# Bringing and summing K and V of the first two batches one batch at a time in a pooled-attention and top-1 MoE kernel

## The chip, the core and the metric

The kernel runs on one core of a Trainium2 chip. Time is device time in microseconds (us) of one execution. The engines are TensorE (PE for matmuls and transposes, PEld for weight loads), VectorE (DVE), ScalarE (ACT), GpSimd (POOL) and SyncE (SP); DMAs are issued from SP, ACT and POOL.

## The reference

```python
# q, k, v: (8 batches, 8 heads, 576 rows, 64)
k_p = k.reshape(B, H, 72, 8, D).mean(axis=3)        # 8 rows become one
v_p = v.reshape(B, H, 72, 8, D).mean(axis=3)
attn = softmax(scale * q @ k_p.transpose(0, 1, 3, 2))
x = (attn @ v_p).transpose(0, 2, 1, 3).reshape(4608, 512)
expert = argmax(x @ w_gate)                         # 8 experts, top-1, limited capacity
out[i] = gate_w[i] * (relu(x[i] @ w1[expert]) @ w2[expert])
```

## The kernel before

**Stages.** The first stage (some 150 us) is attention, in 36 units of work; the rest is the mixture of experts, which the change does not touch. A unit is 256 query rows (two blocks of 128) of four heads. Batch 0 has units 0 to 3, unit 4 holds the last 64 rows of batches 0 and 1 together (the tail unit), units 5 to 8 are batch 1, and so on. The loop over n issues, for unit n: its scores on PE (L476, L479), maximum and subtraction on DVE (L486, L491), the exponential on ACT (L494); for unit n-2: the transposes of its exponentials (L502, copied out by ACT at L503), the products with V (`av`, L516) and their scaling on DVE (`norm`, L525 to L540); for unit n+1 the transposes of its q (`q_part`, L462, copied out at L463). Each engine works through its instructions in the order in which they are written, so an instruction that waits holds up all behind it.

**Pooling K and V.** K and V come for pairs of batches. A pair's 1152 groups of 72 rows lie in 128 partitions, 9 sums to be made in each, and three DMAs of 768 KB bring three sums' rows each (`load_third`). The sums are made by POOL in three additions (`tree`, L370 to L374) or by DVE in one reduction (`red`, L380). For the first pair both engines share them; all later pairs are POOL's. The raw rows lie in 7 buffers.

**Preparing a batch.** `prep_k(b)` transposes the sums of K on PE (L408) into one PSUM bank, and ACT copies them (L417) into `kbs[b % 2]`, which the scores read. `prep_v(b)` does the same for V into `vT` and in a second step multiplies (L438) and masks (L440, L442) into `vbd[b % 2]`, which `av` reads. `turns(n)` says in which unit they are issued: batch 1's K in unit 1 and V in units 2 and 3, batch 2's K in unit 5, V in units 7 and 8.

**The start.** Before unit 0, PE has nothing to do; `busy` gives it products of zeros (L266). K of batches 0 and 1 is summed, batch 0's K prepared, unit 0's q transposed. V's last sums and `prep_v(0)` fall into units 0 to 2. POOL fills its constant tables (`setup`, of which `rest` is the later part) between sums.

**DMA issue.** DMAs from SP and ACT take turns on eight completion semaphores. A ninth DMA is issued only when the one that had its semaphore before has landed. At the start the eight are three of K, one of q, and four small ones of the gate weights (`wgi`, issued from ACT).

Of the kernel before, what the change touches and what calls it, by code (L numbers as in the profile page):

```python
# [31 lines left out]
def pooled_attn_top1_moe(ctx: ExitStack, tc: tile.TileContext, q, k, v, wg, w1, w2, cap, out):  # L32
# [129 lines left out]
    with ExitStack() as actx:  # L162
# [31 lines left out]
        def load_kv(p):  # L194
            raws[p] = [[early_k if p == 1 and src is k and i == 0 else load_third(src, p, i) for i in range(3)] for src in (k, v)]
# [28 lines left out]
        rk = [load_third(k, 0, i) for i in range(3)]  # L224
        qb[0] = ld.tile([P, H, NB, D], F32, name="qblk", tag="qblk")
        rv = []
        for f in range(2):
            hs = slice(f * HH, (f + 1) * HH)
            src = q[0, hs, 0 : NB * P, :].rearrange("h (p j) d -> p h j d", j=NB)
            for j in range(0, NB, 2):  # L230
                nc.sync.dma_start(qb[0][:, hs, j : j + 2], src[:, :, j : j + 2])
                if f == 0:
                    rv.append(load_third(v, 0, j // 2))
            if f == 0:
                rv.append(load_third(v, 0, 2))
        raws[0] = [rk, rv]
        early_k = load_third(k, 1, 0)
# [31 lines left out]
        nc.vector.tensor_copy(wgi[:, :, 0:D], ident[0:D, None, 0:D].to_broadcast([D, NCH, D]))  # L269
# [9 lines left out]
        for i in range(2):  # L279
            nc.vector.tensor_scalar(out=vbd[i][:, :, :, XW - 1 : XW], in0=mk[:, :, :, None], scalar1=float(POOL), scalar2=None, op0=ALU.mult)  # L280
# [109 lines left out]
        def pool(p):  # L390
            for w, dst in (("k", kps[p]), ("v", vps[p])):
                left[w, p] = 3
                for i in range(3):
                    gq.append(tree(dst[:, third(i)], raws[p]["kv".index(w)][i], (w, p)))
                    if p == 1 and w == "k" and i == 0:
                        gq.append(rest)

        def turned(x, b, w, z=None):

            while left.get((w, b // 2)):  # L400
# [342 lines left out]
        with tc.manual_schedule():  # L743
            nc.gpsimd.memset(kbs[1], 0.0)
            z = busy(33)
            rest = setup()
# [488 lines left out]
```

## Time and profile before

| | us |
|---|---|
| median of 3 runs (627.95 to 629.42) | 629.0 |
| the profiled execution | 628.05 |
| its span, first to last instruction | 626.3 |

The profiled execution's time is 1.75 us more than its span. Busy times are shares of the span; a unit of the attention takes 4 to 5 us. In timelines each row is a start, a duration (merged over consecutive instructions of one kind, where x says how many), engine, line, tiles written and read, and in brackets the idle time of the engine before it with what ended it.

### The profile page before, as it was taken

To read this page: it belongs to the slowest core of one execution; us is meant where nothing else is said; L and a number is where in the kernel's file an instruction comes from. 1 tells how busy PE (TensorE), PEld (TensorE's weight loads), DVE (VectorE), ACT (ScalarE), POOL (GpSimd) and SP (SyncE) were. 2 spreads that over 40 slices of the span, in tenths; PEclk is the share of its full clock that TensorE was granted. 3 is DMA by queue.
4 is the path that set the end of the run, shared out by engine and by line. 5 is a ranking of instruction groups with operands and counts; after the bars stand their busy time and mean duration, and the time that the engine had idled before them with its cause. 6 is when DMAs were issued, how large, how long until landed. Compare 5 with 4: busy or idle time off the path is not lost. (4 is left out here: it accounts for less than half of the span.)

```text
span 626.3 us, 14918 instructions
## 1 busy us (share of the span) xinstructions
PE 609.2 (97%) x4249; PEld 549.1 (88%) x4250; DVE 304.2 (49%) x680; ACT 262.2 (42%) x443; POOL 302.1 (48%) x468
## 2 busy tenths in 40 slices
PE   9999999999999999999999999999999999999993
PEld 8889899898898888988888989989899888988982
DVE  4667877978878212168265622118212674112112
ACT  2565576577561212268274522217212582212122
POOL 7799779355644241345544441345414255341344
PEclk9999999999999999999999999999999999999997
DMA  9998963394722520158627820224502271120121
GB/s 322 351 351 305 349 205 115 127 264 146 269 83 71 185 67 14 53 174 310 195 100 273 296 103 5 64 67 139 204 34 67 76 253 40 64 67 18 49 66 51
DMA packets 47084, 93.81 MB, mean 150 GB/s; under 512 B 13392, under 2 KB 23632, under 8 KB 47060
## 3 DMA queue, kind: packets, MB, share of 16 engines
q1 hardware_dynamic: 30836, 60.37, 28.0%
q0 software_dynamic: 11392, 21.57, 11.3%
q10 hardware_dynamic: 4832, 11.56, 5.1%
q8 instruction: 14, 0.23, 0.2%
q14 instruction: 10, 0.08, 0.0%
HBM read 132.97 MB, written 31.27 MB: 262 GB/s over the span
## 5 line engine op out<-in xcount | busy, mean ns | idle before, releaser
L1141 DVE SCALAR_TENSOR_TENSOR hl<-ph,hh 128x512 fp32r<-128x512 f32 x60 | 40.7, 690 | 145.8 <-ACT hh L1140 134.2
L1140 ACT ACTIVATE hh<-ph 128x512 fp32r<-128x512 f32 x60 | 36.0, 599 | 115.8 <-PE ph L150 115.8
L150 PE MATMUL ph<-xh,w1h 128*128 128x256 f32 x480 | 76.4, 282 | 2.4 <-DVE hl L1141 1.8
L150 PE MATMUL ph<-xh,w1l 128*128 128x256 f32 x480 | 75.8, 280 | 0.0
L150 PE MATMUL ph<-xl,w1h 128*128 128x256 f32 x480 | 75.8, 280 | 0.0
L95 POOL DMA_INDIRECT xg<-xs,ix x42 | 45.9, 1094 | 56.7 <-PE y L159 49.2
L159 PE MATMUL y<-w2h,hh 128*128 128x512 f32 x280 | 71.7, 398 | 0.0
L150 PEld LDWEIGHTS ph<-xh,w1h 128*128 128x128 f32 x480 | 65.7, 189 | 4.7 <-DVE hl L1141 2.6
L159 PE MATMUL y<-w2h,hl 128*128 128x512 f32 x280 | 69.3, 390 | 0.0
L159 PE MATMUL y<-w2l,hh 128*128 128x512 f32 x280 | 69.2, 389 | 0.0
L516 PE MATMUL pa<-vbd,pT 96*128 96x146 f32 (+1 forms) x480 | 66.4, 294 | 0.8 <-DVE lt L540 0.8
L150 PEld LDWEIGHTS ph<-xl,w1h 128*128 128x128 f32 x480 | 65.2, 190 | 0.0
L150 PEld LDWEIGHTS ph<-xh,w1l 128*128 128x128 f32 x480 | 64.7, 189 | 0.0
L159 PEld LDWEIGHTS y<-w2l,hh 128*128 128x128 f32 x280 | 52.6, 188 | 11.1
L159 PEld LDWEIGHTS y<-w2h,hl 128*128 128x128 f32 x280 | 52.6, 188 | 10.9
L516 PEld LDWEIGHTS pa<-vbd,pT 96*128 96x128 f32 (+1 forms) x480 | 56.4, 179 | 4.4 <-DVE lt L540 1.9
L100 POOL DMA_INDIRECT out_dram<-zrow,iz x40 | 50.6, 1264 | 15.5 <-issue 15.5
L159 PEld LDWEIGHTS y<-w2h,hh 128*128 128x128 f32 x280 | 49.6, 188 | 9.6 <-ACT hh L125 0.9
L126 DVE TENSOR_TENSOR xl<-px,xh 128x512 fp32r<-128x512 f32 x40 | 25.8, 686 | 60.8 <-ACT xh L125 60.8
L93 POOL TENSOR_TENSOR guard<-ix 128x2 int32<-128x2 int32 x21 | 4.1, 194 | 104.8 <-DVE ix L90 100.4
L125 ACT CAST xh<-px 128x512 fp32r<-128x512 f32 x40 | 21.5, 591 | 73.8 <-PE px L1128 73.5
L676 POOL DMA_INDIRECT slots<-pairs,gix x36 | 35.5, 986 | 33.4 <-DVE pairs L669 19.9
(236 smaller groups left out, 1052.1 us busy)
## 6 DMA issues: line engine op xcount, KB each, us to landing
r<-in_moe_w_dram SPq DMA_DIRECT2D x84, 1024.0 KB, 7.5
raw<-in_k_dram SPq DMA_DIRECT2D x12, 768.0 KB, 9.8
raw<-in_v_dram SPq DMA_DIRECT2D x12, 768.0 KB, 9.5
xs<-xo ACTq DMA_DIRECT2D x16, 512.0 KB, 5.0
qblk<-in_q_dram SPq DMA_DIRECT2D x14, 512.0 KB, 8.5
raw<-in_moe_w_dram SPq DMA_DIRECT2D x4, 512.0 KB, 5.0
r<-in_moe_w_dram ACTq DMA_DIRECT2D x2, 1024.0 KB, 8.5
qblk<-in_q_dram SPq DMA_DIRECT2D x4, 256.0 KB, 8.7
```

Source lines behind the costliest of these rows:

```text
L93: nc.gpsimd.tensor_sub(guard[:, :, 0:1], ix[:, :, 0:1], ix[:, :, 0:1])
L95: nc.gpsimd.indirect_dma_start(out=dst[:, i, :].bitcast(F32), out_offset=None, in_=src, in_offset=bass.IndirectOffsetOnAxis(ap=ix[:, i, 0: ...
L100: ins = nc.gpsimd.indirect_dma_start(out=out[:, :], out_offset=bass.IndirectOffsetOnAxis(ap=i_, axis=0), in_=src, in_offset=None, bounds_c ...
L125: nc.scalar.copy(hi, src)
L126: eng.tensor_sub(lo, src, hi.bitcast(F32))
L150: nc.tensor.matmul(p[:, f2], a[:, c, f * P : (f + 1) * P], b[:, c], start=(f2 == 0 and j == 0 and c == 0), stop=(f2 == 1 and j == 2 and c ...
L159: nc.tensor.matmul(y, a[:, c, i * P : (i + 1) * P], b[:, c], start=(n == 0), stop=(n == 3 * KF - 1))
L516: nc.tensor.matmul(self.pa[us, j, h0 * XW : (h0 + 2) * XW], self.pT[:, j, c, us], vbd[b % 2][:, cc].rearrange("r a x -> r (a x)"), start=( ...
L676: ins = nc.gpsimd.indirect_dma_start(out=slots[:, :], out_offset=bass.IndirectOffsetOnAxis(ap=ix[:, g, 0:1], axis=0), in_=pairs[:, pr + g0 ...
L1140: nc.scalar.activation(hh[s], p, AF.Relu)
L1141: nc.vector.scalar_tensor_tensor(out=hl[s], in0=p, scalar=0.0, in1=hh[s].bitcast(F32), op0=ALU.max, op1=ALU.subtract)
```

## The change

K and V of batches 0 and 1 are loaded and summed per batch. A batch's 64 groups (head and eighth of the rows) have nine sums each; the first eight are laid over 128 partitions, sums 0 to 3 in even and 4 to 7 in odd partitions, in two DMAs of 512 KB, and the ninth lies in 64 partitions, in one DMA of 128 KB. The order of the loads becomes K0, a quarter of q0, V0, a quarter of q0, K1, two quarters of q0, V1. The sums lie in `kps[-2]`, `kps[-1]` for batches 0 and 1, and `turned` and `natural` have a second form for them: three transposes in place of five, three copies in place of two. For batch 0's K, ACT copies partitions 0 to 63 of the bank and DVE partitions 64 to 127. `prep_k(1)` moves from unit 1 to unit 3, `prep_v(1)` from unit 2 to 4, `prep_k(2)` from 5 to 7, `prep_v(2)` from 7 to 8. Two preparations of constants move from DVE to ACT. `rest` goes behind the sums of K and V of batches 2 and 3. The dummy products before unit 0 fall from 33 to 19, and q of unit 0 is transposed ahead of K.

```diff
+        def load_one(src, b):
+            view = src[b].rearrange("h (g r j) d -> (h g) r (j d)", r=NR, j=POOL)
+            four = view[:, 0 : NR - 1].rearrange("q (a r) x -> q a r x", a=2)
+            ts = [kv_tile() for _ in range(2)]
+            for i, t in enumerate(ts):
+                nc.sync.dma_start(t[:, 0:2], four[:, :, 2 * i : 2 * i + 2])
+            nc.sync.dma_start(ts[1][0:GB, 2:3], view[:, NR - 1 :])
+            return ts
...
+        one["k", 0] = load_one(k, 0)
+        load_first_q(0, 0)
+        one["v", 0] = load_one(v, 0)
+        load_first_q(0, 2)
+        one["k", 1] = load_one(k, 1)
+        for j in range(0, NB, 2):
+            load_first_q(1, j)
+        one["v", 1] = load_one(v, 1)
         load_qtail(0)
         load_q(1)
...
-        nc.vector.tensor_copy(wgi[:, :, 0:D], ident[0:D, None, 0:D].to_broadcast([D, NCH, D]))
+        nc.scalar.copy(wgi[:, :, 0:D], ident[0:D, None, 0:D].to_broadcast([D, NCH, D]))
...
+            if b < 2:
+                nc.tensor.transpose(pk[:, 0:P], x[:, 0:2].rearrange("p r d -> p (r d)"), ident)
+                if z is not None:
+                    busy(4, z)
+                nc.tensor.transpose(pk[0:D, 2 * P : 2 * P + GB], x[0:GB, NO], ident[0:GB, 0:GB])
+                nc.tensor.transpose(pk[:, P : 2 * P], x[:, 2:NO].rearrange("p r d -> p (r d)"), ident)
+                return pk
...
+            if b < 2:
+                for o in range(2):
+                    (odd if o else copy)(v[:, :, o : NR - 1 : 2].rearrange("d q (a i) -> d q a i", a=2),
+                                         pk[o * D : (o + 1) * D, 0 : 2 * P].rearrange("d (i q a) -> d q a i", i=2, a=2))
+                copy(v[:, :, NR - 1], pk[0:D, 2 * P : 2 * P + GB])
+                return
...
-            z = busy(33)
+            z = psc.tile([P, HH, 256], F32, name="ps", tag="ps")[:, 0]
+            busy(19, z)
             rest = setup()
...
+            for i in (1, NO):
+                gq.append(tree(*row_of("k", 0, i)))
+            for i in (1, 3, NO):
+                gq.append(tree(*row_of("v", 0, i)))
+            red(*row_of("k", 0, 0))
+            red(*row_of("k", 0, 2, 2))
             drain(gq)
...
             load_kv(1)
+            units[0].q_part()
             prep_k(0, z)
-            units[0].q_part()
+            red(*row_of("v", 0, 0))
...
+                late = 2 if p == 0 else 0
-                if j == 1:
+                if j == 1 + late:
                     prep_k(2 * p + 1)
-                if j == 2:
+                if j == 2 + late:
                     hq.append(prep_v(2 * p + 1))
...
-                    if j == 5:
+                    if j == 5 + late:
                         prep_k(2 * p + 2)
-                    if j == 7:
+                    if j == 7 + late // 2:
                         hq.append(prep_v(2 * p + 2))
...
                 if n == 0:
-                    red(vps[0][:, NR - 1 :], raws[0][1][2][:, 2:3])
+                    red(*row_of("v", 0, 2))
+                    for w in "kv":
+                        pool_one(w, 1, ((0, 2), (2, 2)))
                     pooled(1)
                     pool(1)
+                if n in (1, 2):
+                    red(*row_of("kv"[n - 1], 1, NO))
```

On SP's queue at the very start, the loads of K and V (`raw`), of q (`qblk`) and of the tail rows of q (`qtail`) stood so:

```order
L191 DMA raw<-in_k_dram 128x1536 x3
L231 DMA qblk<-in_q_dram 128x4x128
L191 DMA raw<-in_v_dram 128x1536
L231 DMA qblk<-in_q_dram 128x4x128
L191 DMA raw<-in_v_dram 128x1536 x2
L231 DMA qblk<-in_q_dram 128x4x128 x2
```

and now stand so:

```order
L203 DMA raw<-in_k_dram 128x1x1024 x2
L204 DMA raw<-in_k_dram 64x512
L239 DMA qblk<-in_q_dram 128x4x128
L203 DMA raw<-in_v_dram 128x1x1024 x2
L204 DMA raw<-in_v_dram 64x512
L239 DMA qblk<-in_q_dram 128x4x128
L203 DMA raw<-in_k_dram 128x1x1024 x2
L204 DMA raw<-in_k_dram 64x512
L239 DMA qblk<-in_q_dram 128x4x128 x2
```

Ahead of the last two quarters of q0 stand now K0, V0 and K1 with two quarters; before it was K and V of both batches.

On PE, from the transposes of V of batch 0 (`pk<-identr,vp`) through units 2 and 3 (`ps` scores, `pp` transposed exponentials, `pq` transposed q, `pa` products with V), before:

```order
L408 MATMUL pk<-identr,vp 64x64
L266 MATMUL pv<-zw 128x128 x4
L438 MATMUL pv<-wgi,vT 96x80 x6
L408 MATMUL pk<-identr,kp 128x64 x4
L408 MATMUL pk<-identr,kp 64x64
L479 MATMUL ps<-kbs_146,qT 128x144 x2
L502 MATMUL pp<-identr,pt 96x128 x3
L479 MATMUL ps<-kbs_146,qT 128x144 x2
L502 MATMUL pp<-identr,pt 96x128 x3
L462 MATMUL pq<-identr,qblk 128x128 x4
L516 MATMUL pa<-vbd_148,pT 128x146 x3
L408 MATMUL pk<-identr,vp 128x64 x4
```

and now, from unit 3's `pq` (the tail unit's q) into unit 4's scores, which read K of batch 1 in `kbs_153`:

```order
L509 MATMUL pq<-identr,qtail 128x128 x4
L563 MATMUL pa<-vbd_154,pT 128x146 x3
L433 MATMUL pk<-identr,kp 128x128
L436 MATMUL pk<-identr,kp 64x64
L437 MATMUL pk<-identr,kp 128x128
L563 MATMUL pa<-vbd_154,pT 128x146 x3
L523 MATMUL ps<-kbs_152,qT 64x144
L523 MATMUL ps<-kbs_153,qT 64x144
```

The transposes of batch 1's K stood ahead of unit 2's scores, two units before their first reader; they now stand ahead of the reader with three products between.

On ACT, in units 2 to 4 (`kbs_147` before and `kbs_153` now is batch 1's K, `pt` the exponential), before:

```order
L417 COPY vT<-pk 64x64x4
L494 ACTIVATE pt<-pt 128x576
L417 COPY kbs_147<-pk 64x64x5
L417 COPY kbs_147<-pk 64x64x4
L417 COPY kbs_147<-pk 64x64x5
L417 COPY kbs_147<-pk 64x64x4
L503 COPY pT<-pp 96x384 x2
```

and now:

```order
L550 COPY pT<-pp 96x384 x2
L510 COPY qT<-pq 128x512
L541 ACTIVATE pt<-pt 128x576
L451 COPY kbs_153<-pk 64x64x4 x2
L453 COPY kbs_153<-pk 64x64
L451 COPY kbs_153<-pk 64x64x4 x2
L453 COPY kbs_153<-pk 64x64
L550 COPY pT<-pp 96x384 x2
```

The six copies of batch 1's K stand behind unit 3's exponential.

## Rows read from the trace of the kernel before

**Rows 1.** The page: busy time of each engine, its share of the span and its instructions.

```profile
PE 609.2 (97%) x4249; PEld 549.1 (88%) x4250; DVE 304.2 (49%) x680; ACT 262.2 (42%) x443; POOL 302.1 (48%) x468
```

**Rows 2.** The timeline of the start: POOL's first and last addition for the ninth sums of K, the copies of batch 0's K, DVE's first work on V, unit 0's first scores, POOL's first work on V's third piece, unit 2's q.

```profile
9.74 0.73 POOL L370 TENSOR_TENSOR t<-raw 128x256 f32<-128x256 f32 x1 [0.82 <-DMA raw<-in_k_dram]
...
11.09 0.32 POOL L374 TENSOR_TENSOR kp<-t 128x64 f32<-128x64 f32 x1
...
13.42 1.77 ACT L417 COPY kbs<-pk 64x320 f32<-64x320 f32 x4 [8.00 <-PE pk L408]
...
15.24 2.80 DVE L380 TENSOR_REDUCE vp<-raw 128x192 f32<-128x1536 f32 x1 [2.58 <-DMA raw<-in_v_dram]
...
15.86 1.25 PE L479 MATMUL ps<-kbs,qT 128*128 128x144 f32 x8 [0.54 <-ACT qT L463]
...
18.55 1.27 POOL L370 TENSOR_TENSOR t<-raw 128x512 f32<-128x512 f32 x1 [2.39 <-DMA raw<-in_v_dram]
...
19.52 0.63 PE L462 MATMUL pq<-identr,qblk 128*128 128x128 f32 x4
```

**Rows 3.** Windows: start and end of the stretch, its length, busy time of PE, PEld, DVE, ACT and POOL with their instructions, granted clock, DMA share, and GB/s (the last number).

```profile
0.00:7.37 7.37, 6.21 (x40) 6.23 (x42) 1.20 (x3) 1.60 (x3) 5.28 (x23) 1.00 0.73 253
0.00:9.74 9.74, 8.58 (x61) 8.60 (x63) 3.57 (x4) 1.60 (x3) 6.76 (x24) 1.00 0.82 278
...
0.00:15.24 15.24, 14.08 (x103) 13.39 (x104) 6.50 (x8) 3.36 (x8) 10.83 (x29) 1.00 0.90 319
0.00:18.55 18.55, 16.18 (x117) 15.18 (x119) 9.81 (x10) 4.50 (x9) 11.68 (x30) 1.00 0.93 324
...
0.00:15.00 15.00, 13.84 (x102) 13.27 (x104) 6.50 (x8) 3.14 (x7) 10.59 (x29) 1.00 0.90 317
0.00:16.00 16.00, 14.30 (x104) 13.54 (x106) 7.26 (x9) 3.92 (x8) 11.52 (x30) 1.00 0.90 324
...
0.00:27.00 27.00, 23.98 (x187) 22.15 (x189) 14.95 (x17) 9.76 (x20) 19.55 (x46) 1.00 0.99 324
...
14.00:20.00 6.00, 4.73 (x37) 4.12 (x37) 4.72 (x4) 2.81 (x6) 3.37 (x5) 1.00 1.06 372
...
614.00:626.30 12.30, 2.65 (x12) 1.88 (x10) 0.85 (x4) 1.38 (x2) 6.58 (x9) 0.71 0.21 64
```

**Rows 4.** The timeline of SP's queue: when an issue began and how long the issuing took.

```profile
5.48 0.33 SPq L191 DMA_DIRECT2D raw<-in_v_dram  x1
5.86 0.45 SPq L231 DMA_DIRECT2D qblk<-in_q_dram  x1
9.67 0.81 SPq L191 DMA_DIRECT2D raw<-in_v_dram  x2
```

**Rows 5.** What SP's queue waited for from 0 to 12 us: us in total, times, longest.

```profile
SPq L191 <- DMA wgi<-in_moe_w_gate_dram: 5.5, 2, 3.3
```

**Rows 6.** The timeline from unit 2's scores to unit 4's. In order: unit 2's scores, unit 0's transposed exponentials, transposes of batch 1's V, unit 3's scores, unit 0's scaling (first step), unit 3's maximum, batch 1's V products, unit 3's exponential, unit 4's scores.

```profile
23.91 0.76 PE L479 MATMUL ps<-kbs,qT 128*128 128x144 f32 x4
...
25.26 0.51 PE L502 MATMUL pp<-identr,pt 128*96 128x128 f32 x3 [0.59 <-DVE vbd L442]
...
27.71 0.52 PE L408 MATMUL pk<-identr,vp 64*128 64x64 f32 x5
...
29.00 0.66 PE L479 MATMUL ps<-kbs,qT 128*128 128x144 f32 x4
...
29.20 0.17 DVE L525 TENSOR_SCALAR rz<-pa 128x8 f32<-128x8 f32 x1 [1.36 <-PE pa L516]
...
30.52 0.76 DVE L486 TENSOR_REDUCE mx<-ps 128x8 f32<-128x576 f32 x1
...
31.92 1.24 PE L438 MATMUL pv<-wgi,vT 64*96 64x80 f32 x12
32.18 0.69 ACT L494 ACTIVATE pt<-pt 128x576 f32<-128x576 f32 x1 [0.31 <-DVE pt L491]
...
34.04 0.71 PE L476 MATMUL ps<-kbs,qT 128*64 128x144 f32 x8
```

**Rows 7.** Groups of instructions by line and shape, 0 to 60 us: times, then busy time in us and mean ns of one.

```profile
L380 DVE TENSOR_REDUCE kp<-raw 128x128 f32<-128x1024 f32 x1 | 1.9, 1915 | 0.0
...
L380 DVE TENSOR_REDUCE vp<-raw 128x64 f32<-128x512 f32 x1 | 1.1, 1066 | 0.0
...
L417 ACT COPY kbs<-pk 64x256 f32<-64x256 f32 x6 | 2.5, 419 | 0.1
...
L257 ACT CAST identr<-mats 128x128 fp32r<-128x128 f32 x1 | 0.3, 300 | 0.0
```

**Rows 8.** Windows of the dummy products alone: the stretch, its length, busy time of PE and PEld with their instructions, granted clock, DMA share, GB/s.

```profile
1.00:3.00 2.00, 1.84 (x8) 1.85 (x9) 1.00 0.52 123
3.00:5.00 2.00, 2.00 (x13) 2.00 (x12) 1.00 0.97 347
5.00:7.00 2.00, 2.00 (x21) 2.00 (x20) 1.00 1.03 404
```

**Rows 9.** The timeline of POOL's last two sums of V of batches 2 and 3 (each ends a third), and of PE's transposes of V of batch 2.

```profile
44.03 0.59 POOL L374 TENSOR_TENSOR vp<-t 128x192 f32<-128x192 f32 x1
...
47.54 0.59 POOL L374 TENSOR_TENSOR vp<-t 128x192 f32<-128x192 f32 x1
...
49.68 0.35 PEld L408 LDWEIGHTS pk<-identr,vp 64*128 64x128 f32 x5
```

More of the change, by code (lines that the diff above doesn't have):

```diff
@@ L194, in load_kv @@
         def load_kv(p):
-            raws[p] = [[early_k if p == 1 and src is k and i == 0 else load_third(src, p, i) for i in range(3)] for src in (k, v)]
+            raws[p] = [[load_third(src, p, i) for i in range(3)] for src in (k, v)]
+        def load_one(src, b):
[6 more added lines that the diff above has]
+            return ts
         def load_q(b):
@@ L222, in pooled_attn_top1_moe, with load_first_q @@
         raws, qb, qtl, kps, vps, left = {}, {}, {}, {}, {}, {}
-        rk = [load_third(k, 0, i) for i in range(3)]
         qb[0] = ld.tile([P, H, NB, D], F32, name="qblk", tag="qblk")
-        rv = []
-        for f in range(2):
+        def load_first_q(f, j):
             hs = slice(f * HH, (f + 1) * HH)
             src = q[0, hs, 0 : NB * P, :].rearrange("h (p j) d -> p h j d", j=NB)
[L230 to L237, printed above, removed]
+            nc.sync.dma_start(qb[0][:, hs, j : j + 2], src[:, :, j : j + 2])
+        one = {}
+        one["k", 0] = load_one(k, 0)
[6 more added lines that the diff above has]
+        one["v", 1] = load_one(v, 1)
         load_qtail(0)
@@ L279, in pooled_attn_top1_moe @@
         for i in range(2):
-            nc.vector.tensor_scalar(out=vbd[i][:, :, :, XW - 1 : XW], in0=mk[:, :, :, None], scalar1=float(POOL), scalar2=None, op0=ALU.mult)
+            nc.scalar.activation(vbd[i][:, :, :, XW - 1 : XW], mk[:, :, :, None], AF.Copy, scale=float(POOL))
         def setup():
@@ L394, in pool, with row_of, pool_one, turned @@
                     gq.append(tree(dst[:, third(i)], raws[p]["kv".index(w)][i], (w, p)))
[L395 to L400, printed above, removed]
+            if p == 1:
+                gq.append(rest)
+        NO = NR // 2
+        def row_of(w, b, i, n=1):
+            ts, dst = one[w, b], (kps if w == "k" else vps)[b - 2]
+            if i == NO:
+                return dst[0:GB, NO : NO + 1], ts[1][0:GB, 2:3]
+            return dst[:, i : i + n], ts[i // 2][:, i % 2 : i % 2 + n]
+        def pool_one(w, b, ranges):
+            left[w, b - 2] = len(ranges)
+            for i, n in ranges:
+                gq.append(tree(*row_of(w, b, i, n), (w, b - 2)))
+        def turned(xs_, b, w, z=None):
+            p = b // 2 if b > 1 else b - 2
+            while left.get((w, p)):
                 step(gq)
             pk = bank([P, 512], "pk")
+            x = xs_[p]
+            if b < 2:
[5 more added lines that the diff above has]
+                return pk
             bs = slice((b % 2) * GB, (b % 2 + 1) * GB)
             for i in range(0, NR, 2):
-                if z is not None and i in (2, 6):
-                    busy(i, z)
                 m = min(2, NR - i) * D
@@ L410, in turned, with natural, half @@
             return pk
-        def natural(dst, pk):
+        def natural(dst, pk, b, copy=nc.scalar.copy, odd=nc.scalar.copy):
             v = dst.rearrange("d h (g r) -> d (h g) r", r=NR)
+            if b < 2:
[4 more added lines that the diff above has]
+                return
             for o in range(2):
                 n = (NR + 1 - o) // 2
-                nc.scalar.copy(v[:, :, o : NR : 2], pk[o * D : (o + 1) * D, 0 : n * GB].rearrange("d (i q) -> d q i", q=GB))
+                copy(v[:, :, o : NR : 2], pk[o * D : (o + 1) * D, 0 : n * GB].rearrange("d (i q) -> d q i", q=GB))
         def prep_k(b, z=None):
             ks = kbs[b % 2]
-            pk = turned(kps[b // 2], b, "k", z)
+            pk = turned(kps, b, "k", z)
+            def half(op, mine, its, *a):
+                ins = op(*a).ins
+                tc.add_to_no_dep_group(mine, ins)
+                tc.declare_no_dep(ins, group=its, reason="other partitions of the bank, other rows")
+            two = () if b else (partial(half, nc.scalar.copy, "even", "odd"), partial(half, nc.vector.tensor_copy, "odd", "even"))
             for x in range(2):
-                natural(ks[x * D : (x + 1) * D, x], pk)
+                natural(ks[x * D : (x + 1) * D, x], pk, b, *two)
         def prep_v(b):
             vT = wk.tile([D, H, SP_], F32, name="vT", tag="vT", bufs=1)
-            natural(vT, turned(vps[b // 2], b, "v"))
+            natural(vT, turned(vps, b, "v"), b)
             yield
```

17 lines of the change are left out of this document (5 added, 12 removed).

## The prediction

> **What bounds the kernel now.** First the page: PE is busy 97% of the span [rows 1], so a saving counts if it lets PE go on earlier and PE loses it nowhere later. The change works on the first 60 us only, so I went to the timeline. PE's first useful block, unit 0's scores, begins at 15.86; until then PE works on zeros while K arrives in three pieces, the last at 9.74, goes through sums, transposes and four copies from 13.42 [rows 2]. V's third piece arrives at 18.55, unit 2's q is transposed at 19.52 [rows 2], unit 2's scores begin at 23.91, unit 3's at 29.00, unit 4's at 34.04 [rows 6]. From there units follow each other on a busy PE. So I compare the start of unit 4's scores, which read both batches, before and after, and add what PE work is moved behind that point.
>
> **Supply.** The windows tell what has been moved by a moment: 9.74 x 278 GB/s = 2.71 MB, 15.24 x 319 = 4.86 MB, 18.55 x 324 = 6.01 MB [rows 3]. Due in the order of issue were then K (2.36 MB) at 9.74, K, q and two pieces of V (4.46) at 15.24, all of V and two q pieces (5.24) at 18.55. A piece is thus usable when 0.35, 0.41 or 0.77 MB more than its due has been moved. In the new order a batch's K or V is 1.18 MB and a q piece 0.26.
>
> First K and first q: due 1.44, with 0.35 that is 1.79 MB, reached shortly before 7.37 (1.86 MB) [rows 3], say 7.2. The sums behind are short: POOL's ninth sums took 9.74 to 11.41 [rows 2], DVE two sums 1.92 [rows 7], so 9.1 at the latest. Transposes, then the copies on two engines, ACT's share 2 x (0.42 + 0.30) = 1.44 us: a copy of 256 columns is in [rows 7]; one of 64 columns isn't shown, lies between 0 and 0.42, and I take the 0.30 of the 128-column cast, the nearest row. Unit 0's scores at about 10.9, 5 us earlier. From them to unit 2's q took 19.52 - 15.86 = 3.66 [rows 2], so PE could have that q at 14.6.
>
> That q, however, is now the twelfth DMA on SP and stands behind K1: due 3 x 1.18 + 3 x 0.26 = 4.33 MB. The nearest row is the one at 15.24, so I add its 0.41: 4.73 MB, which is 14.9 (4.76 MB had been moved by 15.0) [rows 3]. One q piece more is in it than before at that point; such stretches moved less, (6.01 - 5.18) MB in 2.55 us after 16.0 against 0.43 in the us before [rows 3], so 0.2 more. T = 15.1, with 0.35 or 0.77 in place of 0.41 14.9 to 16.0. PE waits here half a us, and most of the 5 us is gone: the last word on the start is this q's, 4.4 us earlier than 19.52.
>
> **From T to unit 4.** T to unit 2's scores took 23.91 - 19.52 = 4.39. Five transposes of batch 1's K leave this stretch (they ran between V's products; 0 to 0.52, I take 0.3) and a third copy of V enters, half of whose 0.30 I count as hidden: 4.24. V's sums are ready by then (DVE, behind unit 0's scores: 10.9 + 1.25 [rows 2] + 1.66 from maximum to exponential [rows 6] + 1.07 [rows 7] = 14.9).
>
> Unit 2's scores to unit 0's scaling: 29.20 - 23.91 = 5.29, without V's transposes (0.52) and without PE's wait for `vbd` (0.59), as no K takes a bank in between: 4.18 [rows 6]. Scaling to unit 3's maximum 1.32, maximum to the end of the exponential 32.87 - 30.52 = 2.35 [rows 6]. Between scaling and maximum DVE now has V1's ninth sums: 1.07, the 128-partition row [rows 7]. Behind the exponential ACT has the six copies of K1: 4 x 0.42 + 2 x 0.30 = 2.28. Only then can unit 4's scores begin: T + 4.24 + 4.18 + 1.32 + 1.07 + 2.35 + 2.28 = T + 15.4 = 30.5. PE by itself would have been there earlier: unit 3's scores at T + 4.24 + 5.09 - 0.52 - 0.59 = T + 8.2, and its unit, 34.04 - 29.00 = 5.04 less V's products (1.24) plus K1's transposes (0.5), takes 4.3: T + 12.5. So the moved `prep_k(1)` makes a new wait of 2.9 us on PE in front of the tail unit, with all its queue behind it. Queued behind the copies on ACT are unit 4's `pT` and q copies, which would wait for PE anyway.
>
> Before, batch 1's V was transposed (0.52) and multiplied (1.24) ahead of unit 4; now that comes behind: 1.76. Batch 2's K and V move within later units and cancel out.
>
> **The sum.** 34.04 - 30.5 - 1.8 = 1.7 us less span: 624.6 in place of 626.3, and 626.3 for the profiled execution, whose 628.05 holds 1.75 around the span. The median of the runs is 629.0, so 627.3 for it.
>
> **Edits at nothing.** The two preparations moved to ACT are hidden by ACT's 8.00 us of waiting before the first copies [rows 2]. `rest` and the sums of batches 2 and 3: the first piece of that K has due 7.87 MB, with 0.77 8.63, which is 26.7 (8.75 MB by 27.0) [rows 3]; six thirds at 3.51 (44.03 to 47.54 [rows 9]) end at 47.8. They are used by `prep_v(2)`, which stood at 49.68 in unit 7 and now in unit 8, some 4.3 later less the 1.7 gained: 52. Cover 4 us; without it each us late is a us on PE.
>
> **Two rules of the skill.** The first K of 2.36 MB was there at 9.74 [rows 2]. The Trainium skill (DMA: Bandwidth & Descriptors, Anatomy of one DMA) fits a transfer's time as 2.0 us plus its bytes at 436 GB/s. As an estimate from that page of the Trainium skill the first K would land 7.4 us after its issue near the span's start, and unit 2's q 11.9 us after it; the trace is slower.
>
> TensorE's granted clock is 1.00, the 2.4 GHz level, in 14 to 20 us with PE busy 4.73 of 6.00, and falls to a mean of 0.71 only at the end, with PE busy 2.65 of 12.30 [rows 3]. The first dummy products nevertheless ran slowly, 8 and 13 instructions in two us each against 21 later [rows 8]. The Trainium skill (TensorE: Matmul & The Clock Gate, HAM oscillation) says that a PE which stands waiting for data between bursts is put back to the lower clock and begins the next burst cold. The trace agrees at the end of the span, and shows no case at the start.
>
> **Rivals.**
> Supply is no limit: unit 2's q is there before PE asks at 14.6. Then T = 14.6, gain 2.2, 626.8. For it: small pieces may spread more evenly. Against: 0.35 to 0.77 MB of lag in all rows. The fit of the Trainium skill's page on DMA would lead here too.
>
> The copies don't hold unit 4: if ACT's six copies are done by T + 12.5, the gain is 34.04 - 27.6 - 1.76 = 4.7, 624.3; halfway 625.8. For it: V1's ninth sums or the copies may cost less than the rows of larger shapes. Against: 2.9 us must vanish.
>
> A gap in supply: SP waited 5.5 us for `wgi`, until 5.48 and until 9.67 [rows 4, 5]. Four of the eight semaphores are still `wgi`'s, and now V0's third piece, a q piece and K1 wait on them. Only 1.44 MB are issued ahead, and V0's first two pieces (1.05 MB) behind the first `wgi`. If the second again lands at 9.67, the queue is dry for some 1.5 us: T = 16.6, gain 0.2, 628.8. Beyond T = 18.1 it would be slower. Against: with less K ahead `wgi` should land sooner.
>
> Slower, the clock: PE does 3.1 us of work between 10.9 and T, with two pauses, and 14 dummy products fewer. If the clock falls to its lower level at T, work there runs at half pace, as the start's 21 instructions in 4 us did against 42. Up to unit 3's scores that is up to 8 us; at 4 us lost 629.0 - 1.7 + 4 = 631.3. It decides from 3.0 us lost.
>
> Slower, POOL: if batches 2 and 3 are summed over 4 us later than worked out, by x, the time is 627.3 + x; 630.5 for 3.
>
> **How the numbers follow.** Forecast 0.43, with a range of its own of 626.3 to 628.4 (T from 14.9 to 16.0, the 64-column copy at 0 to 0.42, the transposes at 0 to 0.52). Supply no limit 0.08, no hold by the copies 0.12, gap 0.19, clock 0.10, POOL 0.08. This kernel's measurement tells 0.2% (1.26 us) from no change, so faster means below 627.74: three quarters of the forecast's share and both fast rivals, 0.52; same the rest of the forecast's and most of the gap's, 0.28; slower 0.20. The range of 624.6 to 630.3 leaves out half of the copies' rival, most of the clock's and half of POOL's.
>
> **What would show it.** Unit 0's scores near 11; unit 2's q at 15 with PE idle before it on the DMA of `qblk`; unit 4's scores at 30 to 31 with PE idle some 3 us before them on ACT's `kbs` copies; granted clock 1.00 throughout the start; SP's wait for `wgi` shorter than 3.3 us. The prediction is wrong if PE's wait before unit 4 is missing, if q lands after 16.5, or if PE waits for `kp` or `vp` of batch 2.

## The result and the profile after

The changed kernel takes 634.6 us (median of 4 runs, 633.1 to 636.0); the kernel before 628.5 beside it. The ratio is 1.0095 [1.0067, 1.0123]: slower by 6.1 us, outside the range given (624.6 to 630.3). The profiled execution is the longest of the four, 636.0, with a span 8.0 us longer than before.

The page: the span, the engines' busy time, and the granted clock in 40 slices.

```profile
span 634.3 us, 14839 instructions
...
PE 609.7 (96%) x4205; PEld 549.0 (87%) x4206; DVE 305.3 (48%) x681; ACT 262.3 (41%) x450; POOL 306.5 (48%) x483
...
PEclk9989979999999999999999999999999999999998
```

Against [rows 1] PE is busy 0.5 us longer in a span that is 8 us longer. The page's clock line is the first to look at: the slices near 32 and near 87 us are not full (8 and 7 tenths).

The timeline of the start: q of unit 0, scores of units 0 and 2, unit 2's q ahead of them, ACT's copies of batch 1's K, unit 4's scores.

```profile
8.54 0.63 PE L509 MATMUL pq<-identr,qblk 128*128 128x128 f32 x4 [1.10 <-DMA qblk<-in_q_dram]
...
11.83 1.25 PE L526 MATMUL ps<-kbs,qT 128*128 128x144 f32 x8
...
17.28 0.63 PE L509 MATMUL pq<-identr,qblk 128*128 128x128 f32 x4 [1.70 <-DMA qblk<-in_q_dram]
...
21.95 0.76 PE L526 MATMUL ps<-kbs,qT 128*128 128x144 f32 x4
...
30.23 0.82 ACT L451 COPY kbs<-pk 64x256 f32<-64x256 f32 x2
...
32.18 0.26 ACT L453 COPY kbs<-pk 64x64 f32<-64x64 f32 x1
...
32.50 1.22 PE L523 MATMUL ps<-kbs,qT 128*64 128x144 f32 x6 [2.16 <-ACT kbs L453]
```

Unit 0's scores are 4.0 us earlier than in [rows 2], unit 2's q 2.2, unit 4's scores 1.5 (34.04 in [rows 6]; two of their first eight products ran at 29.88, the other six stand behind the wait). So up to there the change still gains. Unit 4's maximum, which starts behind scores at the lower clock, is only 0.16 us ahead (table below).

Windows, columns as in [rows 3]: five stretches of the start, and three around the dents in the clock.

```profile
0.00:17.28 17.28, 12.64 (x85) 11.67 (x87) 10.07 (x13) 5.24 (x13) 12.98 (x39) 1.00 0.94 271
...
6.00:8.00 2.00, 1.45 (x13) 1.25 (x12) 1.24 (x2) 0.10 (x1) 1.19 (x3) 1.00 1.26 226
8.00:10.00 2.00, 1.46 (x13) 1.47 (x13) 0.87 (x1) 0.58 (x1) 1.13 (x4) 1.00 0.99 397
10.00:12.00 2.00, 2.00 (x17) 1.76 (x16) 1.31 (x3) 1.12 (x4) 1.78 (x4) 1.00 1.15 271
...
14.00:16.00 2.00, 1.25 (x8) 1.03 (x8) 2.00 (x3) 0.96 (x2) 1.86 (x3) 1.00 1.11 291
...
30.00:40.00 10.00, 7.84 (x54) 6.17 (x55) 3.92 (x11) 6.07 (x15) 9.53 (x10) 0.83 1.04 396
80.00:90.00 10.00, 7.89 (x53) 7.28 (x53) 7.41 (x17) 5.04 (x11) 9.27 (x11) 0.84 0.48 160
90.00:100.00 10.00, 10.00 (x80) 9.09 (x79) 5.63 (x15) 4.94 (x10) 9.15 (x13) 0.82 0.20 65
```

Before, the granted clock is 1.00 in all three of these last windows. In each case here the fall to the lower level (1.2 GHz) follows a wait of PE: 2.16 us for `kbs` until 32.50, and 2.11 us until 85.35, the latter new and not foreseen. What PE waited for from 5 to 100 us (total, times, longest):

```profile
PE pq L509 <- DMA qblk<-in_q_dram: 2.8, 2, 1.7
PE ps L523 <- ACT kbs L453: 2.2, 1, 2.2
PE pq L509 <- ACT pT L550: 2.1, 1, 2.1
PE pp L549 <- ACT kbs L457: 1.1, 1, 1.1
```

The wait at 85 leads to DVE. PE stands behind ACT's copy (`pT`), ACT behind unit 13's exponential, and that behind unit 13's maximum on DVE, at 82.73. There the first route (the choice of experts for batches 0 and 1) runs in small steps between the units' maxima. Its end in the kernel before, with unit 12's and unit 13's maxima (`mx`) and POOL's first sum for batches 6 and 7, which waits for unit 12's maximum by a copy (`apart`):

```profile
71.37 0.74 DVE L486 TENSOR_REDUCE mx<-ps 128x8 f32<-128x576 f32 x1
...
72.32 1.81 POOL L370 TENSOR_TENSOR t<-raw 128x768 f32<-128x768 f32 x1
74.21 1.00 POOL L372 TENSOR_TENSOR t<-t 128x384 f32<-128x384 f32 x1
75.29 0.60 POOL L374 TENSOR_TENSOR kp<-t 128x192 f32<-128x192 f32 x1
...
76.26 0.17 DVE L659 TENSOR_SCALAR ghi<-gpos 128x9 f32<-128x9 f32 x1
...
77.03 0.70 DVE L486 TENSOR_REDUCE mx<-ps 128x8 f32<-128x576 f32 x1
```

And in the kernel after:

```profile
74.39 0.74 DVE L533 TENSOR_REDUCE mx<-ps 128x8 f32<-128x576 f32 x1
...
79.32 2.01 DVE L706 TENSOR_SCALAR ghi<-gpos 128x9 f32<-128x9 f32 x1
79.34 0.18 POOL L1081 COPY apart<-mx 128x1 f32<-128x1 f32 x1
79.49 1.80 POOL L382 TENSOR_TENSOR t<-raw 128x768 f32<-128x768 f32 x1
...
81.37 1.02 POOL L384 TENSOR_TENSOR t<-t 128x384 f32<-128x384 f32 x1
81.44 0.97 DVE L709 SCALAR_TENSOR_TENSOR gpos<-gpos,gmm 128x9 f32<-128x9 f32 x1
...
82.73 0.70 DVE L533 TENSOR_REDUCE mx<-ps 128x8 f32<-128x576 f32 x1
```

A step of 0.17 us on nine numbers per partition takes 2.01 and ends with POOL's addition; the next but one takes 0.97 and ends with POOL's second. Before, POOL had finished that sum 0.4 us earlier than the step came. Now POOL is 7.2 us later (its first piece of K of batch 2 at 29.37 in place of 23.81, and `rest`, which had filled waiting time, behind it), DVE only 3. (Each of these sums joins 8 rows; a pair's K has 1152 of them, nine to a partition, so the 72 rows that the section on the kernel before gives to a group are those of a partition.)

Where the 8.0 us of span went, by starts of maxima (table below). Unit 4's scores are 1.54 us ahead; unit 11's maximum is 2.69 behind. The 4.2 lost are 1.76 of work moved behind unit 4, 1.7 of clock (0.17 of the window from 30 to 40), 1.1 of PE's wait for batch 2's K copies, less 0.3 not traced. From unit 11 to 16 another 5.6: 2.7 between units 12 and 13 (8.34 for 5.66), the rest mostly clock (0.16 + 0.18 of two windows are 3.4 in all, not all of which lengthened this stretch). From unit 16 on the distance to the kernel before stays near 8 (7.6 to 8.3), and is 8.05 at the attention's last maximum (175.4 in the kernel before).

### The profile page after: what moved, and what is told of

It reads as the page before. It is cut to its first block, busy times and chain, and to the rows that moved or that the text cites. A ratio compares the mean times of both kernels' runs of the same rounds, so it can differ in the third digit from the quotient of the medians.

```text
span 634.3 us, 14839 instructions
## 1 busy us (share of the span) xinstructions
PE 609.7 (96%) x4205; PEld 549.0 (87%) x4206; DVE 305.3 (48%) x681; ACT 262.3 (41%) x450; POOL 306.5 (48%) x483
## 5 line engine op out<-in xcount | busy, mean ns | idle before, releaser
L159 PE MATMUL y<-w2h,hh 128*128 128x512 f32 x280 | 71.7, 398 | 0.0
L159 PEld LDWEIGHTS y<-w2h,hl 128*128 128x128 f32 x280 | 52.6, 188 | 10.9
L100 POOL DMA_INDIRECT out_dram<-zrow,iz x40 | 47.6, 1191 | 15.8 <-issue 15.8
L550 ACT COPY pT<-pp 96x384 f32<-96x384 f32 x72 | 33.8, 474 | 42.1 <-PE pp L549 39.2
```

Of the source, the lines that this page charges most:

```text
L100: ins = nc.gpsimd.indirect_dma_start(out=out[:, :], out_offset=bass.IndirectOffsetOnAxis(ap=i_, axis=0), in_=src, in_offset=None, bounds_c ...
L159: nc.tensor.matmul(y, a[:, c, i * P : (i + 1) * P], b[:, c], start=(n == 0), stop=(n == 3 * KF - 1))
L550: nc.scalar.copy(self.pT[:, j], pp[0:KC, 0:HC])
```

## The experiments

Starts of six units' maxima on DVE, in us, from the profiled execution of each kernel:

| kernel | unit 4 | 11 | 12 | 13 | 16 | 20 |
|---|---|---|---|---|---|---|
| before | 35.90 | 65.58 | 71.37 | 77.03 | 88.31 | 105.62 |
| after | 35.74 | 68.27 | 74.39 | 82.73 | 96.63 | 113.93 |
| e1_rest_first | 35.70 | 69.09 | 75.37 | 81.03 | 92.34 | 109.64 |
| e2_k1_unit2 | 32.97 | 64.74 | 73.36 | 82.50 | 94.98 | 112.28 |
| e3_fill | 36.92 | 68.73 | 75.35 | 83.29 | 94.17 | 111.47 |
| e4_before_pool_late | 35.89 | 65.54 | 71.22 | 79.41 | 93.31 | 110.61 |
| e5_rest_k1_v1 | 34.02 | 65.17 | 71.53 | 77.35 | 88.65 | 105.75 |
| e6_rest_k1_v1_q | 32.72 | 63.86 | 70.49 | 78.44 | 89.31 | 107.09 |
| e7_rest_fill | 36.09 | 68.40 | 75.11 | 80.94 | 92.87 | 109.97 |
| e8_q | 33.81 | 66.23 | 74.30 | 82.78 | 94.35 | 111.65 |
| e9_hold | 35.32 | 67.69 | 73.79 | 79.49 | 90.71 | 107.94 |
| e10_all_hold | 32.88 | 64.04 | 72.39 | 79.93 | 92.38 | 109.68 |
| e11_hold_v | 32.61 | 63.77 | 70.11 | 77.62 | 90.10 | 107.41 |
| e12_hold_fill | 36.42 | 68.71 | 77.30 | 86.75 | 100.23 | 117.48 |

Times (median, lowest to highest, beside the kernel before on the same chip, and the ratio with its interval). Five of the kernels ran on a chip on which the kernel before took 640 to 641 us:

| kernel | us | before | ratio |
|---|---|---|---|
| e1 | 631.4 (629.7 to 634.7) | 628.1 | 1.0062 [1.0035, 1.0089] |
| e2 | 634.0 (632.9 to 635.4) | 628.1 | 1.0091 [1.0064, 1.0118] |
| e3 | 635.6 (632.8 to 639.2) | 628.1 | 1.0139 [1.0095, 1.0182] |
| e4 | 632.7 (631.1 to 633.1) | 628.1 | 1.0067 [1.0043, 1.0091] |
| e8 | 634.6 (633.6 to 635.4) | 627.9 | 1.0106 [1.0089, 1.0123] |
| e9 | 633.1 (631.0 to 639.8) | 627.9 | 1.0113 [1.0069, 1.0158] |
| e10 | 634.4 (632.2 to 637.4) | 627.9 | 1.0105 [1.0083, 1.0126] |
| e5 | 644.1 (641.0 to 646.6) | 641.3 | 1.0036 [1.0013, 1.0059] |
| e6 | 644.2 (641.0 to 647.5) | 641.3 | 1.0058 [1.0035, 1.0080] |
| e7 | 645.0 (642.8 to 648.0) | 641.3 | 1.0055 [1.0033, 1.0077] |
| e11 | 642.8 (641.7 to 644.4) | 640.2 | 1.0049 [1.0032, 1.0067] |
| e12 | 644.4 (642.0 to 650.1) | 640.2 | 1.0072 [1.0044, 1.0100] |

The theory: POOL's additions hold up those small steps of DVE, PE waits behind DVE, and the clock falls behind PE's waits; the wait before unit 4 does the same on its own. The chief rival: the start, thinner in dummy products, or supply alone.

**POOL earlier: e1_rest_first.**

```diff
+            if p == 1:
+                gq.append(rest)
             for w, dst in (("k", kps[p]), ("v", vps[p])):
...
-            if p == 1:
-                gq.append(rest)
```

> POOL's constants (`rest`, 5.85 us at 50.43 in the trace of after) go ahead of the sums of K and V of batches 2 and 3, into the 4.23 us in which POOL waits for that K. Theory (POOL's additions are late and hold up the small DVE steps of the first route): POOL is some 4.2 us ahead at 73, the route's L706 and L709 take 0.2 us each in place of 2.01 and 0.97, PE's 2.11 us of waiting at 85.35 goes, and so does the lower granted clock from 86.8 on; 634.6 - 2.7 - 2.7 = 629.2 us. The first stretch of lower clock at 32.2 stays. Rival (the loss past unit 10 has nothing to do with POOL, but with PE's own order or the clock alone): L706 may shorten, yet 633 to 635. Rival (POOL's last V sums of batches 2 and 3, now 1.6 us later at 52.1, are late for PE): a new wait on `vp` near 56, 1 us more.

The timeline of e1_rest_first, and below it its windows:

```profile
76.33 1.80 POOL L382 TENSOR_TENSOR t<-raw 128x768 f32<-128x768 f32 x1
...
80.27 0.17 DVE L706 TENSOR_SCALAR ghi<-gpos 128x9 f32<-128x9 f32 x1
```

```profile
30.00:40.00 10.00, 7.82 (x41) 5.95 (x41) 2.64 (x6) 4.99 (x13) 9.32 (x16) 0.66 1.04 397
...
80.00:90.00 10.00, 10.00 (x90) 9.13 (x88) 8.12 (x22) 7.25 (x15) 7.89 (x9) 1.00 0.46 159
```

The stall and the second fall are gone: units 12 to 13 take 5.66 as before, unit 16 comes 4.3 us earlier than in after. No new wait on `vp`. From unit 12 to unit 16 it takes 16.97 us, against 22.24 in after and 16.94 in the kernel before. The time fell by less than forecast, to 631.4 for 629.2. In the profiled execution (631.2) the first fall lasted longer, 0.66 of full clock in 30 to 40 against 0.83, which is 1.7 us; that the other runs lost theirs in the same way is not shown.

**The same lateness given to the kernel before: e4_before_pool_late.**

```diff
+                    for _ in range(11):
+                        nc.gpsimd.iota(spos, pattern=[[0, E], [P, MT]], base=0, channel_multiplier=1, allow_small_or_imprecise_dtypes=True)
                     nc.gpsimd.tensor_copy(apart, early["mx"][:, 0, 0:1])
```

> The kernel before, with eleven needless fillings of a POOL constant (0.41 us each, 1.05 us of them in POOL's idle time) ahead of its first sum for batches 6 and 7, so that this sum starts near 75.6 in place of 72.3 and lies over the first route's small steps at 76.26. Theory: the step of 0.17 us takes 1 us or more, the next ones too, PE waits up to 2 us behind them and the granted clock falls for some us: 628.5 + 2.5 to 5.5 = 631 to 634. Rival (POOL's additions do not hold DVE; the match in the trace of after is by chance): 628.5, since POOL has 5.83 us of idle time behind that sum.

Its timeline: the eleven fillings, POOL's addition, two steps of the route, PE's wait; then the window.

```profile
70.34 5.07 POOL L1029 IOTA spos<- 128x288 f32 x11
...
75.51 1.80 POOL L370 TENSOR_TENSOR t<-raw 128x768 f32<-128x768 f32 x1
75.60 1.80 DVE L652 TENSOR_TENSOR gps<-gps,oh 128x64 f32<-128x64 f32 x1
...
77.70 0.72 DVE L659 TENSOR_SCALAR ghi<-gpos 128x9 f32<-128x9 f32 x1
...
82.03 0.66 PE L462 MATMUL pq<-identr,qblk 128*128 128x128 f32 x4 [1.96 <-ACT pT L503]
```

```profile
80.00:90.00 10.00, 8.04 (x40) 7.28 (x39) 5.72 (x14) 5.14 (x11) 9.29 (x11) 0.66 0.28 98
```

POOL had time to spare, yet 3.2 us of lateness cost 5.0 us at unit 16 and 4.6 us of time: 2.5 between units 12 and 13 (8.19 for 5.66), the rest mostly clock. This kernel has nothing of the change, so the start isn't needed for the loss. With e1 this decides for the theory as far as the stall at the route goes.

**Only the hold: e9_hold.** After, with POOL as late as ever, but its sum waiting for the next unit's maximum.

```diff
-                    nc.gpsimd.tensor_copy(apart, early["mx"][:, 0, 0:1])
                     setup_rows()
+                if n == 3 * NB + 1:
+                    nc.gpsimd.tensor_copy(apart, early["mx"][:, 0, 0:1])
                     pooled(3)
...
-                step(gq, 3 if n == 3 * NB else 4 if n <= n_early else 2 if n in (n_early + 1, n_early + 4) else 0 if n == n_early + 3 else 1)
+                step(gq, 3 if n in (3 * NB, 3 * NB + 1) else 4 if n <= n_early else 2 if n in (n_early + 1, n_early + 4) else 0 if n == n_early + 3 else 1)
```

> After, with one edit: POOL's first sum for batches 6 and 7 is held until unit 13's maximum (it waited for unit 12's), so that no addition of POOL can lie over the route's steps L706 to L716; POOL is as late as in after otherwise. Theory (those additions alone make the stall at the first route): L706 and L709 take 0.2 us each, unit 13's maximum comes 2.5 to 2.9 us earlier than in after (near 80), PE's 2.11 us at 85 and the lower clock from 86.8 go: 634.6 - 2.7 - 2.7 = 629.2 us, with the first clock stretch still there. Rival (POOL's lateness acts in another way too, by the scatters or by sums that are late): less than half of that, 632 or more.

The step that took 2.01 us, in e9_hold's timeline:

```profile
78.72 0.17 DVE L706 TENSOR_SCALAR ghi<-gpos 128x9 f32<-128x9 f32 x1
```

From unit 12's maximum to unit 13's it takes 5.70 us in place of 8.34, from unit 12's to unit 16's 16.92, as in the kernel before (16.94), and unit 16's comes 5.9 us earlier than in after; the profiled run takes 631.0. So POOL's lateness acts by this meeting and by nothing else up to there. The median is 633.1, since the four runs differ more than any kernel's so far: mean granted clocks of 0.993, 0.992, 0.989 and 0.982 for 631.0, 631.5, 634.6 and 639.8 us. By the times alone e9 can't be told from after (1.0113 [1.0069, 1.0158] against 1.0095 [1.0067, 1.0123]), and the median lies where the rival put it. What e9 shows, it shows by the trace, up to unit 16.

**The wait before unit 4: e2_k1_unit2 and e3_fill.**

```diff
-                if j == 1 + late:
+                if j == 1 + late // 2:
                     prep_k(2 * p + 1)
```

> Only K of batch 1 is prepared a unit earlier, in unit 2 instead of unit 3. Theory: its sums are there (DVE's last at 24.4, POOL's earlier), ACT's six copies are done before unit 4's scores; PE's 2.16 us of waiting at 32.50 and the 3.4 us of lower clock behind it go, the granted clock is 1.00 in 30 to 40; 634.6 - 2.2 - 1.4 = 631.0. Rival: the wait is only moved, PE stands in unit 2 or 3 behind the same copies, 633.5 to 635. Rival (the start alone is to blame, by fewer dummy products): no change, 634.6. The stall at the first route stays in any case, unless the earlier units move it against POOL.

The wait and the first fall are gone, 2.8 us at unit 4 and 3.5 at unit 11, as forecast. But PE now comes to the first route while POOL is still on V of batches 4 and 5; e2_k1_unit2's timeline:

```profile
69.57 1.80 POOL L382 TENSOR_TENSOR t<-raw 128x768 f32<-128x768 f32 x1
69.62 1.78 DVE L661 TENSOR_TENSOR oh<-cw,gmm 128x8 fp32r<-128x8 f32 x1
...
72.62 1.02 PE L563 MATMUL pa<-vbd,pT 96*128 96x146 f32 x6 [2.97 <-DVE lt L587]
```

Its granted clock is 0.68 in 70 to 80. Nearly all is given back, 634.0. The forecast of 631.0 took the later stall as it was; the exception that the expectation named is what came: a PE that is earlier against POOL makes it worse.

```diff
+                    if self is units[NB]:
+                        busy(22, self.ps[:, 0])
```

> The wait before unit 4's scores stays, but PE fills it with 22 products of zeros (some 2.1 us at the higher clock). Theory (PE's idle time before the tail unit is what the first lower clock follows): granted clock 1.00 in 30 to 40, unit 5 starts some 1.4 us earlier; 634.6 - 1.4 = 633.2. Rival (the clock falls for another reason, as the thinner start): 0.83 in 30 to 40 as now, and 634.6 to 635. The stall at the first route and the lower clock from 86.8 stay by both.

A product counts as two instructions, so the fill took 5.08 us instead of 2.1, and unit 4 came 1.2 us later. The clock stayed at 1.00 from 30 to 40 us all the same, as the theory has it, but the time did not fall: 635.6 for the 633.2 forecast. In this profile it also stayed up after PE's 1.7 us of waiting at the first route, but the other three runs have 0.990, 0.990 and 0.988: the falls don't come in every execution. e7_rest_fill and e12_hold_fill repeat it with 11 products on top of the cures of e1 and e9.

> e1_rest_first, and PE's wait before unit 4's scores filled with 11 products of zeros (22 instructions of 0.115 us by the rate of e3_fill, 44 in 5.08 us; 2.5 us in all). In e3_fill they took 5.08 us, longer than the wait. Theory (the first lower clock follows PE's idle time there): granted clock 1.00 in 30 to 40, unit 5's maximum near 40.2 to 40.5 in place of 41.8 in e1_rest_first, no stretch of lower clock before the end, and runs that lie closer together than 629.7 to 634.7; 629.7 us. Rival (the clock's falls do not hang on that wait): a stretch at the lower clock all the same, and 631.4.

> e9_hold, and PE's wait before unit 4's scores filled with 11 products of zeros, as in e7_rest_fill. What is left of after's loss is then the wait itself. Theory (the falls of the clock follow PE's waits): no lower clock near 32, unit 5's maximum 0.5 to 1.4 us earlier than in e9_hold's profile, and runs that lie closer than e9_hold's 631.0 to 639.8; 630.0 us. Rival (the falls do not hang on this wait): a stretch at the lower clock near 32 in most runs and the same spread, 633.

Neither has a fall near 32 us. So in the four profiles that have this wait unfilled (after, e1, e8, e9) the clock fell there, and in the three that have it filled it did not. e7's unit 5 comes at 40.62, near the forecast, though its q came late and its start is 1.7 us behind; e7's clock fell only at 174.5, e12's already at 17.9, where PE waited for q, and again at the route: the steps L644 and L663 (L642 and L661 of after) took 1.68 and 1.78 us under POOL's additions for V of batches 4 and 5, which the hold doesn't touch; PE waited 2.9 us, and the clock fell for 13.7 us from 75.9 on. The expectations for their times failed: the spread stayed.

**Supply: e8_q.**

```diff
+        load_first_q(1, 0)
         one["k", 1] = load_one(k, 1)
-        for j in range(0, NB, 2):
-            load_first_q(1, j)
+        load_first_q(1, 2)
```

> After, with unit 2's q ahead of K of batch 1 on SP's queue. Theory (T, unit 2's q, is set by what is queued ahead of it): transposed near 15.6 in place of 17.28, unit 4's scores 1.0 to 1.7 us earlier. What that is worth at the end depends on where POOL then meets the first route: 633 if it stays as it is; POOL is later against PE by as much as PE is earlier. Rival (T is not set by the queue ahead of it): 17 or more, and no change up to unit 4.

Unit 2's q is transposed at 15.89, without a wait, and unit 4's scores begin 1.4 us earlier, still behind the copies (2.15 us). At the first route L661 took 1.78 and L706 1.76 us, the clock was at its lower level for 6.8 us from 76.0 on, behind 2.4 us of PE's waiting, and the whole lead was gone by unit 13 (82.78 for 82.73).

**All cures together: e5, e6, e10, e11.** e5 is e1 with e2, and one pair of V1's sums made by DVE; e6 adds e8's order; e10 adds e9's hold; e11 also holds POOL's last third of V of batches 4 and 5.

```diff
-                    for w in "kv":
-                        pool_one(w, 1, ((0, 2), (2, 2)))
+                    pool_one("k", 1, ((0, 2), (2, 2)))
+                    pool_one("v", 1, ((0, 2),))
...
+                if n == 3:
+                    red(*row_of("v", 1, 2, 2))
```

In e11, where POOL's sums of batches 4 and 5 are queued, and behind e9's copy of `apart`:

```diff
                         pool(p + 2)
+                        held.append(gq.pop())
...
+                    gq.extend(held)
```

> Three edits of after at once: `rest` ahead of the sums of batches 2 and 3, K of batch 1 prepared in unit 2, and the second pair of V1's sums made by DVE (1.9 us, in unit 3) in place of POOL (2.5 us). Theory: the wait before unit 4 goes (unit 4's maximum at 33.0 as in e2_k1_unit2, 2.8 us earlier than in after), and POOL, 2.5 us less laden than in e1_rest_first, is waiting for unit 12's maximum when it comes, as in the kernel before, so that the route's small steps take 0.2 us and no lower clock follows; PE's attention ends 2.8 + 4.3 us or more earlier than in after: 634.6 - 7.1 = 627.5, or 626 if the clock stays up throughout. Rival (POOL is still late against an earlier PE, as in e2_k1_unit2): steps of 1 us or more at the first route, a wait on `lt` or `pT` and a clock stretch, 630 to 633.

> The same as e5_rest_k1_v1, and unit 2's q comes ahead of K of batch 1 on SP's queue in place of behind it. Theory (the thin gain at the start is unit 2's q, held up behind K1): that q is transposed near 15.6, when PE asks for it, in place of 17.3, and the 1.7 us come back in every later unit if K1's sums, some 1 us later, still hold nothing up: e5 less 1.0 to 1.7 us. Rival (the start moves, but K1's sums, V1 or POOL set the end of the first units): unit 4's maximum within 0.5 us of e5's, and the same time.

> e6_rest_k1_v1_q with the hold of e9_hold. Theory: as e6 up to unit 12 (maximum 0.9 us ahead of the kernel before), then without e6's 2.3 us at the first route, 1 to 1.5 us ahead of the kernel before in units 13 to 20; the later routes stay open, since POOL and PE meet there anew: 0.998 of the time before if they cost nothing, 627.0 where before is 628.1. Rival (every unit that PE gains only moves the meeting of POOL's additions and DVE's small steps to another place): a stall of 1 us or more at the second or third route, and 1.000 to 1.005.

> e10_all_hold, and POOL's last third of V of batches 4 and 5 (68.61 to 72.15 there) is held until unit 13's maximum too, so that it can't lie over the first route's L661 (1.78 us). Theory (every addition of POOL that lies over a small step of DVE costs, and only these): L661 takes 0.2 us, L642 and L645 still meet the third before it, PE's wait for `lt` falls from 2.7 to some 1 us and no stretch of lower clock follows near 74; unit 13's maximum at 78 or earlier, unit 20's 0.5 to 2 us earlier than in the kernel before at best; 0.998 to 1.002 of the time before. Rival (POOL's sums are then late for their readers): a wait on `vp` or `kp` in units 16 to 23, 1.005.

e5 loses nothing at the first route (5.82 us from unit 12 to 13), stays at full clock to 110 us and reaches unit 20 at 105.75: 8.2 us earlier than after, and level with the kernel before, not ahead of it. e6 is 1.7 us ahead of the kernel before at unit 11 and 1.5 behind at unit 20: the route cost 7.95 us for 5.66. e10 frees the route's last steps, and meets POOL in the first ones; its timeline:

```profile
68.61 1.80 POOL L382 TENSOR_TENSOR t<-raw 128x768 f32<-128x768 f32 x1
68.65 1.78 DVE L661 TENSOR_TENSOR oh<-cw,gmm 128x8 fp32r<-128x8 f32 x1
```

In e11 that step takes 0.15 us, under one of POOL's fillings in place of an addition:

```profile
67.95 0.41 POOL L335 IOTA spos<- 128x288 f32 x1
68.00 0.15 DVE L661 TENSOR_TENSOR oh<-cw,gmm 128x8 fp32r<-128x8 f32 x1
```

PE's wait fell to 0.7, yet the clock fell all the same at 71.7, and unit 20 is 1.8 us behind. The rival of e10 holds in its mechanism: each gain of PE moves the meeting, here to the first route's first steps and not to a later route, and at 1.0105 it cost more than the 1.005 that the rival allowed. None of the twelve beats the kernel before. On the chip of e5, e6, e7, e11 and e12 the time after unit 32 can't be compared with the other traces: in e5 PE and ACT both stand still there. ACT's 3.7 us are put down to `remote`, something outside the engines of the core; PE's are put down to nothing (what PE waited for in 105 to 200 us):

```profile
PE pp L549 <- issue: 3.9, 2, 3.7
```

## Why the prediction was wrong

**Supply, T = 15.1: failed by its size.** T came at 17.28, later than the 16.5 that the prediction named as a sign that it is wrong. Unit 0's scores came at 11.83 for 10.9. The lag held: 17.28 x 271 GB/s = 4.68 MB had been moved for 4.33 due, 0.35 more, the lower of the three lags. What failed was to take the rate from a trace of before. There q pieces ran beside 768 KB pieces; now a q piece often moves nearly alone (from 6 to 8 us 956 of 1014 packets are smaller than 2 KB, from 8 to 10 only 16 of 210), and the stretches with q run at 226, 271 and 291 GB/s against 397 in the one without. I had allowed 0.2 us for that. Not all of the shortfall is q's: by 4 us, before any q moved, 0.42 MB had come where 0.62 came before (104 and 154 GB/s); why is open. (The fit that the prediction takes from the Trainium skill is given there for DMAs issued from GpSimd, and these are issued from SP; its 11.9 us for this q were 16.4, from the first issue at 0.85 to 17.28.) The gap rival was not it: SP waited 1.9 and 0.8 us for `wgi` (5.5 in [rows 5]), and the DMA engines are busy throughout from 3.5 us on.

**From T to unit 4, 15.4: right.** 32.50 - 17.28 = 15.22, by the steps named, with 2.16 us of PE's wait where 2.9 was forecast. The copies took 2 x 0.41 and 0.26 us per half. The rival of copies that don't hold is refuted.

**The moved work, 1.76: right, but not all.** Batch 2's K copies did not cancel out; PE waited 1.1 us for them.

**The sum: its last step failed.** With 17.28 for T the prediction's own sum gives a loss of 0.4 us in place of a gain of 1.7, some 629.4, still inside the range. What took the time out of it is the last step, which took unit 4's lead, less the moved work, for the whole kernel's. From there the changed kernel lost 4.2 us by unit 11 and 5.6 more by unit 16. Three things were missing. First, a wait I had priced at 2.9 us also cost 1.7 of clock; my clock rival had the mechanism, but put it "at T", where the clock stayed at 1.00. Second, POOL's lateness was priced only by the reader of its sums. Batch 2's K came at 29.37 for the 26.7 worked out, and the sums ended at 50.5 for 47.8; that cover held all the same (`prep_v(2)` reads at 56.0), and the rival of late sums is refuted. But POOL's additions also stop DVE, at a place where nobody reads those sums. e1, e4 and e9 show that by itself: 2.5 to 2.7 us from unit 12 to 13. Third, the clock behind that. By the mean granted clock of the four runs, 0.988 to 0.991, against 0.994 in the profile of before, some 2 x 0.0045 x 633 = 5.7 us more were spent at the lower level, an estimate of 2.8 us of the 6.1 lost.

The trace of before had the sign. The route's step L598 by its line's view (shortest, median, longest in ns, first and last start, forms):

```profile
L598 DVE SCALAR_TENSOR_TENSOR gme<-gd,cw x6: 182/212/1034, 67.7 to 186.4; 128x72 f32<-128x72 f32 x3, 128x24 f32<-128x24 f32 x2, 128x32 f32<-128x32 f32 x1
```

On the same shape, 128x72, it took 0.96 and 1.03 us beneath one of POOL's additions, ending within 0.1 us of it, and 0.23 with no addition beside it: that is a step that is being held. The Trainium skill (SBUF — State Buffer, Who interferes with whom) says that a DVE instruction with two inputs in SBUF contends with a GpSimd one that reads SBUF, the loser standing still for the whole instruction, and that a reduction doesn't. The trace agrees: L661 with two inputs, 1.78 us under an addition and 0.15 without; DVE's sums of V, reductions over 128x512, 1.05 under an addition (at 14.58) and 1.03 over 64 partitions with POOL idle (at 27.05). L706, the step held longest, has one tensor input, so that sentence doesn't cover it; that it is held is shown by after, e4 (L659 there), e8, e1 and e9. By that rule the lateness of POOL was a rival that I should have priced.

## What to carry to other kernels

When a change makes an engine later, ask not only who reads its results, but whom it stops while it works: lay its instructions over the small steps of the engine that shares a path with it, before and after. In a kernel whose bound engine is nearly full, price each new wait of that engine with the clock behind it, in after 1.7 and 3.4 us for two waits of 2. And read rates of transfers from a stretch with the same mix of sizes, not from the mean.

## What the runs showed of the hardware

- POOL's addition over 128x768 holds some DVE steps on 128x8 or 128x9 for as long as it runs: 1.78 us for 0.15, 2.01 for 0.17, even where the step's recorded start is 0.17 us ahead of the addition's. Others run on: in after L573, with one input, took 0.20 at 66.88 beneath an addition from 66.84 to 68.65. POOL's fillings of constants left DVE's steps beneath them as they were (L661 above, 0.15; in e4 a reduction of 0.69 as elsewhere).
- The granted clock fell after waits of PE of 2 us in most profiles, after 0.7 in e11, and not after 1.7 in e3's profile and in e6's, nor after 2.2 for q in e7's. What decides is open.
- One chip ran all kernels, the kernel before too, 2% longer. In its five traces, and in none of the nine others, ACT stands near unit 33 for 3.6 to 3.9 us that the profile puts down to `remote`, and PE for 2.2 to 3.8. That is less than the 12 to 13 us by which the chip is longer; the cause is open, and was not pursued.
- Whether an order of POOL's work exists that lets the earlier start through is open too. A hold of two thirds of V was not tried.
